# Dense mixture in steps of 768 tokens, with sums of block products formed in PSUM

## The chip, the cores and the metric

One core of a Trainium2 chip (trn2). The metric is the time of one execution on the device in microseconds (us); the median of three runs of the kernel before is 754.18 us (754.17 to 754.35). Five engines work side by side, each through its own queue in program order, and wait for each other by semaphores: TensorE (PE, matmuls), VectorE (DVE), ScalarE (ACT), GpSimd (POOL) and SyncE (SP, which issues transfers). PEld is the load of the stationary operand of a matmul. PE writes only to PSUM, which has eight banks of 512 f32 values for each of 128 partitions; DVE and ACT read it from there.

## The reference

Three layers in a row on 1536 tokens of 512 numbers: an attention with a local window and a few global keys, a mixture of 8 experts in which each token goes to one, and a dense mixture, in which each token goes through all 4 experts. The change touches the last one alone:

```python
def _moe2_ref(x, domain_probs, w1, w2):          # x 1536x512, w1 4x512x1024, w2 4x1024x512
    p = domain_probs / (domain_probs.sum(-1, keepdims=True) + 1e-09)
    out = np.zeros((N, D), dtype=np.float32)
    for e in range(E):
        h = np.maximum(x @ w1[e], 0.0)
        out += p[:, e:e + 1] * (h @ w2[e])
    return out
```

## The kernel before, in words

Everything runs in the order in which it is written; the whole body is under a hand-made schedule. The dense mixture begins at L770.

**Exactness.** A product of two f32 matrices is made of three matmuls on numbers split into a high part (rounded to fp32r) and a low part, the rest: high x high, high x low, low x high (`mm3`, L108 to L111). Every operand is therefore split: ACT copies the high part, and DVE or POOL subtracts it (`sub_lo`, L68).

**First layer by seven products.** The hidden layer is computed in 16 quarters: q counts them, q // 4 is the expert, and a quarter has 256 of its 1024 hidden units. For one quarter, the 512 x 256 weights are cut into four blocks A11, A12, A21, A22, and the tokens (two halves of 768) by the two halves of the 512 features into four blocks as well. Instead of eight block products, seven are made (Strassen's scheme in Winograd's form), from sums S1 to S4 of weight blocks and sums T1 to T4 of token blocks. The products are A11 B11, A12 B21, S4 B22, A22 T4, S1 T1, S2 T2, S3 T3. The kernel after numbers them 1 to 7 in this order, and the texts below use these numbers. Each product is 6 matmuls (`product`, L829: three matmuls for each of two halves of the features). The sums that need all tokens' blocks (T1 to T4) are made once, by `prep_a` to `prep_d` (L797 to L827), in the first steps; the sums of weights (S1 to S4) for each q by POOL (`sums_moe2`, L596), and the weights are split by `split_moe2` (L604): ACT makes the high parts, POOL the low ones, for "a" (the A blocks), "s" (their sums) and "w" (second layer).

**Steps.** A step takes one quarter q and one column c of 256 tokens of each half, so 512 tokens: 42 matmuls of 256 columns. There are 16 x 3 = 48 steps (L861). In the first six, c is the outer loop and q alternates between 0 and 1, so that tokens can be prepared as they are needed: tiles 2 and 3 in step 1, tiles 4 and 5 in step 3 (`preps`, L862). From step 6 on q is the outer loop.

**What a step does** (L880 to L956): four products go into `pf` and three into `pg` (two PSUM tiles of two banks each). ACT copies three of the products to SBUF (`sf`, L896), DVE forms `uv`, the sums `cc` (L897, L898, L914, L923), ACT makes the high part of the positive values `hh` (L938) and DVE their low part `hl` (L939). Between the products PE makes the second layer of the step before it (`second`, L837): four times 6 matmuls of 512 columns, each a tile of 128 tokens, whose result is added to the output with its share by DVE (L857), or, for q = 0, written by ACT (L855). In steps 0 to 5 all seven products come first (L32), then the second layer of the step before.

**Weights.** Two sets of buffers alternate by q (L594). After the last step of q the A blocks of q + 2 are fetched into its buffers and summed by POOL (L953 to L955); one step later they are split, in the middle of that step, right behind `uv` and `cc` (L899 to L902), and two steps later the second layer's weights "w".

Of the kernel before, what the change touches and what calls it, by code (L numbers as in the profile page):

```python
# [8 lines left out]
F32 = mybir.dt.float32  # L9
# [5 lines left out]
ALU = mybir.AluOpType  # L15
# [16 lines left out]
ORDERS = {i: ((0, 1, 3, 2, 4, 5, 6) if i % 2 else (0, 4, 1, 3, 2, 5, 6), ()) for i in range(6)}  # L32
# [12 lines left out]
def attention_moe_moe(ctx: ExitStack, tc: tile.TileContext, qkv, nints_d, wg, w1, w2, dprob, u1, u2, out):  # L45
# [62 lines left out]
    def mm3(o, ah, al, bh, bl, start, stop):  # L108
        nc.tensor.matmul(o, ah, bh, start=start, stop=False)  # L109
        nc.tensor.matmul(o, ah, bl, start=False, stop=False)  # L110
        nc.tensor.matmul(o, al, bh, start=False, stop=stop)  # L111
# [658 lines left out]
    with ExitStack() as c2:  # L770
# [6 lines left out]
        sf = placed("sf", [P, 3, 256], F32, 0)  # L777
        uv = placed("uv", [P, 256], F32, 3072)
        cc = placed("cc", [P, 4, 256], F32, 4096)
        hhs = [placed(f"hh{n}x", [P, 4, 256], F32R, 8192 + 8192 * n) for n in range(2)]  # L780
        hls = [placed(f"hl{n}x", [P, 4, 256], F32R, 12288 + 8192 * n) for n in range(2)]
# [47 lines left out]
        def product(o, buf, a, b, c):  # L829
            cs = slice(c * 256, (c + 1) * 256)  # L830
            n = (a % 4) * 256
            lo, hi = (buf[0][1], buf[3][1]) if a < 4 else (buf[2][1], buf[4][1])
            for d in range(2):
                wc = slice(n + d * P, n + (d + 1) * P)
                mm3(o, hi[:, wc], lo[:, wc], xh[:, b, d, cs], xl[:, b, d, cs], d == 0, d == 1)

        def second(q, c, hs, n):  # L837
            buf = bufs2[q % 2]
            hh, hl = hs
            ac = next_pa()  # L840
            half, k = divmod(n, 2)
            tc_ = slice(k * P, (k + 1) * P)
            tt = half * NI + 2 * c + k
            e = q // NQ
            nc_ = 2 if (q, c, n) == (NQ * E2 - 1, 2, 3) else 1
            for j in range(nc_):
# [3 lines left out]
                for fh in range(2):  # L850
                    i = 2 * fh + half
                    wc = slice(fh * 512 + cs.start, fh * 512 + cs.stop)
                    mm3(ac[:, cs], hh[:, i, tc_], hl[:, i, tc_], buf[5][1][:, wc], buf[1][1][:, wc], fh == 0, fh == 1)
# [7 lines left out]
        steps = [(q, c) for c in range(3) for q in range(2)] + [(q, c) for q in range(2, NQ * E2) for c in range(3)]  # L861
# [18 lines left out]
        for i, (q, c) in enumerate(steps + [(None, None)]):  # L880
            tt = nc.vector.tensor_tensor
            order = ORDERS.get(i, ((0, 1, 2, 3), (4, 5, 6)))
            js = preps.get(i)
            if q is not None:
                buf = bufs2[q % 2]
                pf = ps.tile([P, 4, 256], F32, name="pf")
                pg = ps.tile([P, 3, 256], F32, name="pg")
                hh, hl = hhs[i % 2], hls[i % 2]
                prods = [(pf[:, 0], A11, B11), (pf[:, 1], S1, T1), (pf[:, 2], S3, T3), (pf[:, 3], S2, T2),
                         (pg[:, 0], A12, B21), (pg[:, 1], S4, B22), (pg[:, 2], A22, T4)]  # L890
                for n in order[0]:
                    if i == 0 and n == 1:
                        for _ in range(NFILL):
                            nc.tensor.matmul(pf[:, 1], wz[:, 0:P], wz, start=True, stop=True)
                    product(prods[n][0], buf, *prods[n][1:], c)
                nc.scalar.activation(out=sf, in_=pf[:, 0:3], func=AF.Copy)  # L896
                tt(out=uv, in0=pf[:, 3], in1=sf[:, 0], op=ALU.add)  # L897
                tt(out=cc[:, 3], in0=sf[:, 1], in1=sf[:, 2], op=ALU.add)  # L898
                for d, what in ((2, "w"), (1, "as")):  # L899
                    if i >= d and steps[i - d][1] == 2 and steps[i - d][0] + 2 < NQ * E2:  # L900
                        for wh in what:
                            split_moe2(bufs2[steps[i - d][0] % 2], wh, ("A", "G"))  # L902
            if js:
                prep_b(js[0])
                prep_c1(js[0])
                prep_c2(js[0], nc.gpsimd)
                prep_t4(js[0])
            if pend is not None:
                second(*pend, 0)
                second(*pend, 1)  # L910
            if q is not None:
                for n in order[1]:
                    product(prods[n][0], buf, *prods[n][1:], c)
                tt(out=cc[:, 0:3], in0=pg, in1=sf, op=ALU.add)  # L914
            if js:
                prep_b(js[1])
                prep_c1(js[1])
                prep_c2(js[1], nc.gpsimd)
                prep_t4(js[1])
            last = i == len(steps) - 1  # L920
            for n, (what, engs) in enumerate(PD):
                if n == 1 and q is not None and not last:
                    tt(out=cc[:, 1:4], in0=cc[:, 1:4], in1=uv.unsqueeze(1).to_broadcast([P, 3, 256]), op=ALU.add)  # L923
                for j, eng in zip(js or (), engs):
                    prep_d(j, what, eng)
            if i + 1 in preps:
                for t in (preps[i + 1][0], preps[i + 1][0] + NI):
                    prep_a(t)
            if last:
# [10 lines left out]
            if i == 2:  # L940
                gather_x(5 + NI)
# [224 lines left out]
```

## Time and profile before

| | before |
|---|---|
| median of the runs | 754.18 us |
| the profiled execution: time | 756.36 us |
| the profiled execution: span, first to last instruction | 754.6 us |
| PE busy | 98% of the span |
| DVE, ACT, POOL busy | 69%, 41%, 33% |
| share of the dense mixture | from about 239 us to the end |

The rows of the trace are of one profiled execution, with times in us from the start of its span; its time is 1.8 us longer than the span and 2.2 us longer than the median of the runs without a profile. A busy PE is one with a matmul on its way: the records of two neighbouring matmuls overlap, so how fast they follow each other is read from their starts, not from their durations. The granted clock (PEclk) is the share of full speed that TensorE was given in a stretch: 1.00 is its level of 2.4 GHz, 0.5 that of 1.2 GHz.

### The profile page before, as it was taken

To read this page: it belongs to the slowest core of one execution; us is meant where nothing else is said; L and a number is where in the kernel's file an instruction comes from. 1 tells how busy PE (TensorE), PEld (TensorE's weight loads), DVE (VectorE), ACT (ScalarE), POOL (GpSimd) and SP (SyncE) were. 2 spreads that over 40 slices of the span, in tenths; PEclk is the share of its full clock that TensorE was granted. 3 is DMA by queue.
4 is the path that set the end of the run, shared out by engine and by line. 5 is a ranking of instruction groups with operands and counts; after the bars stand their busy time and mean duration, and the time that the engine had idled before them with its cause. 6 is when DMAs were issued, how large, how long until landed. Compare 5 with 4: busy or idle time off the path is not lost.

```text
span 754.6 us, 12189 instructions
## 1 busy us (share of the span) xinstructions
PE 736.4 (98%) x4794; PEld 657.3 (87%) x4794; DVE 522.1 (69%) x1024; ACT 312.7 (41%) x489; POOL 252.8 (33%) x244
## 2 busy tenths in 40 slices
PE   8999998999999999999999999999999999999996
PEld 7999997777777898899999999999999999999995
DVE  7777863678769888576666666676666666666665
ACT  4878861687855544513223132232222322213110
POOL 5666631000046604724414244141341523415000
PEclk8999996999999999999999999999999999999999
DMA  6867602999931300200001000010000100011013
GB/s 163 277 220 247 215 21 86 387 364 405 342 103 54 99 16 28 84 29 29 29 29 56 29 29 29 29 56 29 30 29 29 56 28 29 34 38 43 1 43 129
DMA packets 36018, 74.87 MB, mean 99 GB/s; under 512 B 15960, under 2 KB 16216, under 8 KB 35954
## 3 DMA queue, kind: packets, MB, share of 16 engines
q1 hardware_dynamic: 34034, 69.39, 26.7%
q0 software_dynamic: 1920, 4.64, 1.9%
q8 instruction: 39, 0.64, 0.3%
q14 instruction: 25, 0.20, 0.1%
HBM read 65.19 MB, written 10.49 MB: 100 GB/s over the span
## 4 chain that ended last, share of the span: by engine, by line
PE 87%; DVE 5%; DMA 3%; issue 2%; ACT 2%; POOL 0%; POOLq 0%; ACTq 0%; DVEq 0%
PE pf L110 6%; PE pf L109 6%; PE pf L111 6%; PE pg L109 4%; PE pg L110 4%; PE pg L111 4%; PE pa0x L111 3%; PE pa0x L109 3%; PE pa1x L110 3%; PE pa0x L110 3%; PE pa1x L109 3%; PE pa3x L109 3%; PE pa3x L111 3%; PE pa1x L111 3%; PE pa3x L110 3%; PE pa2x L111 3%
## 5 line engine op out<-in xcount | busy, mean ns | idle before, releaser
L914 DVE TENSOR_TENSOR cc<-pg,sf 128x768 f32<-128x768 f32 x48 | 45.9, 957 | 57.0 <-PE pg L111 55.6
L896 ACT ACTIVATE sf<-pf 128x768 f32<-128x768 f32 x48 | 39.0, 813 | 107.5 <-PE pf L111 107.5
L938 ACT ACTIVATE hh0x<-cc 128x1024 fp32r<-128x1024 f32 x24 | 25.5, 1060 | 120.5 <-DVE cc L923 117.8
L938 ACT ACTIVATE hh1x<-cc 128x1024 fp32r<-128x1024 f32 x23 | 24.4, 1060 | 106.6 <-DVE cc L923 106.6
L599 POOL TENSOR_TENSOR w6x<-w4x 128x256 f32<-128x256 f32 x8 | 9.4, 1178 | 175.1 <-DMA w4x<-in_u_dram 93.2
L923 DVE TENSOR_TENSOR cc<-cc,uv 128x768 f32<-128x768 f32 x47 | 52.5, 1117 | 1.6
L939 DVE SCALAR_TENSOR_TENSOR hl0x<-cc,hh0x 128x1024 fp32r<-128x1024 f32 x24 | 29.5, 1231 | 24.8 <-ACT hh0x L938 24.8
L939 DVE SCALAR_TENSOR_TENSOR hl1x<-cc,hh1x 128x1024 fp32r<-128x1024 f32 x23 | 28.5, 1241 | 25.0 <-ACT hh1x L938 25.0
L897 DVE TENSOR_TENSOR uv<-pf,sf 128x256 f32<-128x256 f32 x48 | 20.4, 424 | 34.1 <-ACT sf L896 34.1
L110 PE MATMUL pf<-xl,r8x 128*128 128x256 f32 x144 | 40.8, 283 | 2.7 <-DVE xl L68 2.5
L857 DVE SCALAR_TENSOR_TENSOR xr<-pa2x,pr,xr 128x512 f32<-128x512 f32 x44 | 33.0, 750 | 13.4 <-PE pa2x L111 13.4
L109 PE MATMUL pf<-xh,r8x 128*128 128x256 f32 x144 | 40.6, 282 | 0.0
L111 PE MATMUL pf<-xh,r6x 128*128 128x256 f32 x144 | 40.4, 281 | 0.0
L109 PE MATMUL pf<-xh,r14x 128*128 128x256 f32 x144 | 40.4, 281 | 0.0
L110 PE MATMUL pf<-xl,r14x 128*128 128x256 f32 x144 | 40.4, 281 | 0.0
L111 PE MATMUL pf<-xh,r12x 128*128 128x256 f32 x144 | 40.4, 281 | 0.0
L599 POOL TENSOR_TENSOR w12x<-w10x 128x256 f32<-128x256 f32 x8 | 8.9, 1119 | 92.6 <-DMA w10x<-in_u_dram 92.6
L857 DVE SCALAR_TENSOR_TENSOR xr<-pa1x,pr,xr 128x512 f32<-128x512 f32 (+1 forms) x46 | 33.9, 737 | 2.2 <-PE pa1x L111 2.2
L857 DVE SCALAR_TENSOR_TENSOR xr<-pa0x,pr,xr 128x512 f32<-128x512 f32 (+1 forms) x46 | 33.9, 736 | 1.2 <-PE pa0x L111 1.2
L857 DVE SCALAR_TENSOR_TENSOR xr<-pa3x,pr,xr 128x512 f32<-128x512 f32 x45 | 33.5, 744 | 0.6 <-PE pa3x L111 0.6
L110 PEld LDWEIGHTS pf<-xl,r8x 128*128 128x128 f32 x144 | 27.0, 188 | 3.4 <-issue 2.5
L68 POOL TENSOR_TENSOR r11x<-w11x,r15x 128x1024 fp32r<-128x1024 f32 x7 | 17.0, 2424 | 35.8 <-ACT r15x L97 35.8
(1189 smaller groups left out, 2700.2 us busy)
## 6 DMA issues: line engine op xcount, KB each, us to landing
w4x<-in_u_dram SPq DMA_DIRECT2D x8, 512.0 KB, 3.2
w5x<-in_u_dram SPq DMA_DIRECT2D x8, 512.0 KB
w10x<-in_u_dram SPq DMA_DIRECT2D x8, 512.0 KB, 3.9
w11x<-in_u_dram SPq DMA_DIRECT2D x8, 512.0 KB, 3.4
qk1x<-in_qkv_dram SPq DMA_DIRECT2D x6, 512.0 KB, 4.7
vv<-in_qkv_dram SPq DMA_DIRECT2D x12, 256.0 KB, 4.9
out_dram<-xr SPq DMA_DIRECT2D x11, 256.0 KB, 2.0
qk0x<-in_qkv_dram SPq DMA_DIRECT2D x5, 512.0 KB, 4.2
```

Of the source, the lines that this page charges most:

```text
L68: eng.tensor_tensor(out=lo, in0=src, in1=hi.bitcast(F32), op=ALU.subtract)
L109: nc.tensor.matmul(o, ah, bh, start=start, stop=False)
L110: nc.tensor.matmul(o, ah, bl, start=False, stop=False)
L111: nc.tensor.matmul(o, al, bh, start=False, stop=stop)
L599: eng.tensor_tensor(out=sm[:, 0], in0=a21, in1=a22, op=ALU.add)
L857: nc.vector.scalar_tensor_tensor(out=acc[:, tt, cs], in0=ac[:, cs], scalar=pr[:, tt, e:e + 1], in1=acc[:, tt, cs], op0=ALU.mult, op1=ALU.add)
L896: nc.scalar.activation(out=sf, in_=pf[:, 0:3], func=AF.Copy)
L897: tt(out=uv, in0=pf[:, 3], in1=sf[:, 0], op=ALU.add)
L914: tt(out=cc[:, 0:3], in0=pg, in1=sf, op=ALU.add)
L923: tt(out=cc[:, 1:4], in0=cc[:, 1:4], in1=uv.unsqueeze(1).to_broadcast([P, 3, 256]), op=ALU.add)
L938: nc.scalar.activation(out=hh, in_=cc, func=AF.Relu)
L939: nc.vector.scalar_tensor_tensor(out=hl, in0=cc, scalar=0.0, in1=hh.bitcast(F32), op0=ALU.max, op1=ALU.subtract)
```

## The change: what it does

From step 6 on a step takes 384 tokens of each half in place of 256, so 768 in all: 28 such steps in place of 42, two for each q. The first six steps keep 256. Each has the same seven products of 6 matmuls, now 256 or 384 columns wide, and a second layer of four or six times 6 matmuls of 512 columns.

The four PSUM tiles are used differently. Products 1, 6, 7 and 4 are added up in one bank (two such banks, by turns of the step), 5 and 3 in another, 2 has one of its own. After 1, after 5 and after 6 ACT copies the bank as it stands (`part`); after 3, 7 and 2 DVE adds a copy to the bank as it stands; after 4 the bank itself is the result. As each quarter of the hidden values is known, ACT makes its high part (`high`), and DVE its low part one piece of work later (`lows`). A product that adds to a bank can only start when the reader of the bank before it is done.

The order of a step is written as a string: digits are products, "s" one sixth or one fourth of the second layer of the step before, "p" the preparation of one tile of tokens, "f" eight matmuls that fill a gap. The splits of the weights now stand behind the whole string of a step.

```diff
-ORDERS = {i: ((0, 1, 3, 2, 4, 5, 6) if i % 2 else (0, 4, 1, 3, 2, 5, 6), ()) for i in range(6)}
+WC = 3 * P
+SEQS = {0: "12f56374", 1: "1563pss724pss", 2: "12s56s37s4s", 3: "1563pss724pss", 4: "12s56s37s4s", 5: "15s63s72s4s", 6: "12s56s37s4s"}
+SEQ = "15s63ss72s4ss"
...
+        banks = [ps.tile([P, 512], F32, name=f"pb{n}x") for n in range(4)]
+        parts = xp.tile([P, 3, WC], F32, name="parts")
...
-        def second(q, c, hs, n):
+        def second(q, tok, w, hs, n):
...
-            half, k = divmod(n, 2)
+            half, k = divmod(n, w // P)
+            half = 1 - half
...
-        steps = [(q, c) for c in range(3) for q in range(2)] + [(q, c) for q in range(2, NQ * E2) for c in range(3)]
+        MS = {1: (A11, B11), 2: (A12, B21), 3: (S4, B22), 4: (A22, T4), 5: (S1, T1), 6: (S2, T2), 7: (S3, T3)}
+
+        class Step:
+            def __init__(self, i, q, tok, w, last):
+                self.buf, self.cs, self.late = bufs2[q % 2], slice(tok, tok + w), []
+                x, y, z = banks[i % 2], banks[2], banks[3]
+                self.bank = {n: b[:, 0:w] for n, b in ((1, x), (6, x), (7, x), (4, x), (2, y), (5, z), (3, z))}
+                self.part, self.cc, self.hs = parts[:, :, 0:w], ccs[w], hps2[w][i % 2]
+
+            def high(self, half, fs, src):
+                nc.scalar.activation(out=self.hs[0][:, half, fs], in_=src, func=AF.Relu)
+                self.late.append((half, fs, src))
+
+            def lows(self, late):
+                for half, fs, src in late:
+                    nc.vector.scalar_tensor_tensor(out=self.hs[1][:, half, fs], in0=src, scalar=0.0, in1=self.hs[0][:, half, fs].bitcast(F32),
+                                                   op0=ALU.max, op1=ALU.subtract)
...
+            def mul(self, n):
+                o, part, cc = self.bank[n], self.part, self.cc
+                late = self.take()
+                product(o, self.buf, *MS[n], self.cs, n in (1, 2, 5), True)
+                add = lambda j, p: nc.vector.tensor_tensor(out=cc[:, j], in0=o, in1=part[:, p], op=ALU.add)
+                if n in (1, 5, 6):
+                    nc.scalar.activation(out=part[:, (1, 5, 6).index(n)], in_=o, func=AF.Copy)
+                elif n == 3:
+                    add(0, 2)
+                elif n == 7:
+                    add(1, 1)
+                    self.high(1, slice(0, 2), cc[:, 0:2])
+                elif n == 2:
+                    add(2, 0)
+                    self.high(0, 0, cc[:, 2])
+                else:
+                    self.high(0, 1, o)
+                self.lows(late)
+
+        steps = [(q, c * 256, 256, c == 2) for c in range(3) for q in range(2)]
+        steps += [(q, c * WC, WC, c == 1) for q in range(2, NQ * E2) for c in range(2)]
...
+        for i, st in enumerate(steps + [None]):
+            js = list(preps.get(i, ()))
+            fs = list(range(2 * pend[2] // P)) if pend else []
+            step = st and Step(i, *st)
+            for m in SEQS.get(i, SEQ) if st else "s" * len(fs):
+                if m == "s":
+                    late = step.take() if st else []
+                    second(*pend, fs.pop(0))
+                    if st:
+                        step.lows(late)
+                elif m == "f":
...
+                elif m == "p":
+                    j = js.pop(0)
+                    prep_b(j)
+                    prep_c1(j)
+                    prep_c2(j, nc.gpsimd)
+                    prep_t4(j)
+                    if not js:
+                        for what, engs in PD:
+                            for j, eng in zip(preps[i], engs):
+                                prep_d(j, what, eng)
+                else:
+                    step.mul(int(m))
+            if st:
+                step.lows(step.take())
                 for d, what in ((2, "w"), (1, "as")):
-                    if i >= d and steps[i - d][1] == 2 and steps[i - d][0] + 2 < NQ * E2:
+                    if i >= d and steps[i - d][3] and steps[i - d][0] + 2 < NQ * E2:
                         for wh in what:
                             split_moe2(bufs2[steps[i - d][0] % 2], wh, ("A", "G"))
...
+            for n, t in enumerate(preps.get(i + 1, ())):
+                if (i, n) == (2, 1):
+                    gather_x(5 + NI)
+                prep_a(t)
+                prep_a(t + NI)
             if i == 8:
                 count(xp, next_pa()[:, 0:E1])
...
+            if pend and pend[0] + 2 < NQ * E2 and steps[i - 1][3]:
+                fetch_moe2(pend[0] + 2, bufs2[pend[0] % 2], "w")
+            if st:
+                q, tok, w, last = st
+                if last and q + 2 < NQ * E2:
+                    fetch_moe2(q + 2, step.buf, "a")
+                    sums_moe2(step.buf, nc.gpsimd)
+                pend = (q, tok, w, step.hs)
```

## Rows read from the trace of the kernel before

**Rows 1.** The page's busy time by engine: us (share of the span) and instructions.

```profile
PE 736.4 (98%) x4794; PEld 657.3 (87%) x4794; DVE 522.1 (69%) x1024; ACT 312.7 (41%) x489; POOL 252.8 (33%) x244
```

**Rows 2.** Busy time by stretch: the stretch, its length, busy us of PE, PEld, DVE, ACT, POOL (instructions), granted clock, share of the DMA engines, GB/s.

```profile
340.00:720.00 380.00, 380.00 (x2413) 345.62 (x2413) 248.85 (x331) 101.19 (x121) 120.45 (x94) 1.00 0.10 33
...
748.00:754.60 6.60, 0.00 (x0) 0.00 (x0) 0.28 (x1) 0.00 (x0) 0.00 (x0) 0.72 0.26 88
```

**Rows 3.** What PE waited for from 238 us to the end: us in total, times, longest us.

```profile
PE pf L110 <- DVE xl L68: 2.5, 3, 0.9
PE pa1x L281 <- DVE t40x L821: 0.5, 1, 0.5
```

**Rows 4.** ACT's reads of the first PSUM tile in steps 9 and 47, from the timeline: start us, duration us, and in brackets the idle time before and what ended it.

```profile
340.08 0.81 ACT L896 ACTIVATE sf<-pf 128x768 f32<-128x768 f32 x1 [2.74 <-PE pf L111]
...
734.77 0.81 ACT L896 ACTIVATE sf<-pf 128x768 f32<-128x768 f32 x1 [2.56 <-PE pf L111]
```

**Rows 5.** The timeline within step 13: the first of twelve 512-wide matmuls, ACT's read of the tile that PE has just finished, the first of eighteen 256-wide matmuls, and the first 512-wide one after them.

```profile
381.37 0.39 PE L109 MATMUL pa1x<-r9x,hh0x 128*128 128x512 f32 x1
...
381.63 0.81 ACT L896 ACTIVATE sf<-pf 128x768 f32<-128x768 f32 x1 [2.22 <-PE pf L111]
...
384.09 0.28 PE L109 MATMUL pg<-xh,r7x 128*128 128x256 f32 x1
...
386.21 0.39 PE L109 MATMUL pa3x<-r9x,hh0x 128*128 128x512 f32 x1
```

**Rows 6.** PE's timeline in step 2, from the first of twelve 256-wide matmuls soon after a wait to the 512-wide one behind them; and in step 3 two groups of four transposes, 128 columns wide.

```profile
264.72 0.28 PE L109 MATMUL pg<-xh,r8x 128*128 128x256 f32 x1
...
266.08 0.39 PE L109 MATMUL pa0x<-r15x,hh1x 128*128 128x512 f32 x1
...
276.48 0.60 PE L281 MATMUL pa0x<-ident,xr 128*128 128x128 f32 x4
276.92 0.60 PE L281 MATMUL pa1x<-ident,xr 128*128 128x128 f32 x4
```

**Rows 7.** Groups of equal instructions: line, engine, operation, out<-in, count, busy us, mean ns of one, idle us before. DVE from 335 to 700 us, and ACT's reads of 512 and of 256 columns from 235 to 330 us.

```profile
L914 DVE TENSOR_TENSOR cc<-pg,sf 128x768 f32<-128x768 f32 x36 | 34.5, 958 | 49.3 <-PE pg L111 47.9 <-PE pa2x L233 1.4
L857 DVE SCALAR_TENSOR_TENSOR xr<-pa1x,pr,xr 128x512 f32<-128x512 f32 x35 | 26.0, 742 | 0.0
L939 DVE SCALAR_TENSOR_TENSOR hl0x<-cc,hh0x 128x1024 fp32r<-128x1024 f32 x18 | 22.1, 1226 | 20.3 <-ACT hh0x L938 20.3
L897 DVE TENSOR_TENSOR uv<-pf,sf 128x256 f32<-128x256 f32 x35 | 14.9, 425 | 24.4 <-ACT sf L896 24.4
...
L808 ACT ACTIVATE xh<-pa1x 128x512 fp32r<-128x512 f32 x5 | 3.0, 598 | 5.6 <-PE pa1x L281 5.4 <-PE pa1x L239 0.2
...
L826 ACT ACTIVATE xh<-t40x 128x256 fp32r<-128x256 f32 x3 | 1.2, 408 | 0.4 <-DVE t40x L821 0.4
```

**Rows 8.** The timeline of the first steps: PE at the wait in step 0, the last high part (ACT) and the last low part (DVE) of the tokens prepared ahead of step 0, and the first matmul of steps 1 to 5.

```profile
243.21 0.38 PE L110 MATMUL pf<-xl,r8x 128*128 128x256 f32 x1 [0.70 <-DVE xl L68]
...
243.86 0.42 ACT L826 ACTIVATE xh<-t41x 128x256 fp32r<-128x256 f32 x1
...
245.12 0.41 DVE L68 TENSOR_TENSOR xl<-t41x,xh 128x256 fp32r<-128x256 f32 x1
...
247.20 0.39 PE L109 MATMUL pf<-xh,r13x 128*128 128x256 f32 x1
...
260.05 0.28 PE L109 MATMUL pf<-xh,r7x 128*128 128x256 f32 x1
...
271.53 0.28 PE L109 MATMUL pf<-xh,r13x 128*128 128x256 f32 x1
...
283.73 0.28 PE L109 MATMUL pf<-xh,r7x 128*128 128x256 f32 x1
...
295.27 0.28 PE L109 MATMUL pf<-xh,r13x 128*128 128x256 f32 x1
```

**Rows 9.** ACT's timeline in step 5: the high parts of A (two pieces) and of S for q = 2, and the evacuation of the last second product of the step.

```profile
299.06 0.93 ACT L97 ACTIVATE r7x<-w4x 128x512 fp32r<-128x512 f32 x2
299.89 1.05 ACT L97 ACTIVATE r8x<-w6x 128x1024 fp32r<-128x1024 f32 x1
...
305.85 0.69 ACT L855 ACTIVATE xr<-pa3x,pr 128x512 f32<-128x512 f32 x1 [0.50 <-PE pa3x L111]
```

**Rows 10.** POOL's groups from 297 to 325 us (columns as in rows 7): the low parts of S and of the two pieces of A for q = 2; and PE's first matmul of step 6 from the timeline.

```profile
L68 POOL TENSOR_TENSOR r6x<-w6x,r8x 128x1024 fp32r<-128x1024 f32 x1 | 2.4, 2402 | 0.0
...
L68 POOL TENSOR_TENSOR r4x<-w4x,r7x 128x256 fp32r<-128x256 f32 x1 | 1.5, 1460 | 0.1
L68 POOL TENSOR_TENSOR r4x<-w4x,r7x 128x512 fp32r<-128x512 f32 x1 | 1.3, 1302 | 3.1 <-PE pg L111 3.1
...
305.65 0.28 PE L109 MATMUL pf<-xh,r7x 128*128 128x256 f32 x1
```

**Rows 11.** Busy time by stretch in the attention layer (columns as in rows 2; the granted clock is the third number from the end).

```profile
112.50:116.00 3.50, 3.24 (x17) 3.14 (x17) 1.50 (x9) 0.00 (x0) 0.00 (x0) 0.51 0.30 78
116.00:119.00 3.00, 2.39 (x12) 1.58 (x11) 1.43 (x9) 0.12 (x1) 0.19 (x1) 0.50 0.00 0
119.00:126.00 7.00, 6.47 (x31) 6.41 (x32) 1.82 (x13) 0.48 (x1) 2.19 (x3) 0.50 0.04 14
```

More of the change, by code (lines that the diff above doesn't have):

```diff
@@ L106, in attention_moe_moe, with mm3 @@
     SCH_M1 = [("A", "V")]
[L108 to L111, printed above, removed]
+    def mm3(o, ah, al, bh, bl, start, stop, **kw):
+        nc.tensor.matmul(o, ah, bh, start=start, stop=False, **kw)
+        nc.tensor.matmul(o, ah, bl, start=False, stop=False, **kw)
+        nc.tensor.matmul(o, al, bh, start=False, stop=stop, **kw)
     ordered = ExitStack()
@@ L776, in attention_moe_moe @@
         t4 = [xp.tile([P, 2, P], F32, name=f"t4{n}x") for n in range(2)]
[L777 to L781, printed above, removed]
+        banks = [ps.tile([P, 512], F32, name=f"pb{n}x") for n in range(4)]
+        parts = xp.tile([P, 3, WC], F32, name="parts")
+        places = {256: (3072, 11264), WC: (20480, 4608)}
+        ccs = {w: placed(f"cc{w}x", [P, 3, w], F32, 0) for w in places}
+        hps2 = {w: [[placed(f"h{m}{n}{w}x", [P, 2, 2, w], F32R, places[w][n] + 16 * w * (m == "l")) for m in "hl"] for n in range(2)] for w in places}
         acc = xr
@@ L827, in prep_d, with product @@
             sub_lo(eng, xl[:, ps_, :, c], src, xh[:, ps_, :, c])
-        def product(o, buf, a, b, c):
-            cs = slice(c * 256, (c + 1) * 256)
+        def product(o, buf, a, b, cs, start, stop):
             n = (a % 4) * 256
@@ L879, in attention_moe_moe @@
         pend = None
[L880 to L898, printed above, removed]
+        for i, st in enumerate(steps + [None]):
[9 more added lines that the diff above has]
+                elif m == "f":
+                    for _ in range(NFILL):
+                        nc.tensor.matmul(banks[3][:, 0:256], wz[:, 0:P], wz, start=True, stop=True)
+                elif m == "p":
[12 more added lines that the diff above has]
+                step.lows(step.take())
@@ L908, in attention_moe_moe @@
[L908 to L929, printed above, removed]
-                for n in (2, 1):
-                    rows = slice(2 - n, 4, 2)
-                    us = slice(2, 3) if n == 2 else slice(1, 4, 2)
-                    tt(out=cc[:, us], in0=cc[:, us], in1=uv.unsqueeze(1).to_broadcast([P, 3 - n, 256]), op=ALU.add)
-                    nc.scalar.activation(out=hh[:, rows], in_=cc[:, rows], func=AF.Relu)
-                    second(*pend, 4 - n)
-                    nc.vector.scalar_tensor_tensor(out=hl[:, rows], in0=cc[:, rows], scalar=0.0, in1=hh[:, rows].bitcast(F32), op0=ALU.max, op1=ALU.subtract)
-            elif q is not None:
-                nc.scalar.activation(out=hh, in_=cc, func=AF.Relu)
-                nc.vector.scalar_tensor_tensor(out=hl, in0=cc, scalar=0.0, in1=hh.bitcast(F32), op0=ALU.max, op1=ALU.subtract)
```

33 lines of the change are left out of this document (7 added, 26 removed).

## The prediction

> **What bounds the kernel now.** I read the page's busy shares first: TensorE (PE) is busy for 98% of the span, VectorE (DVE) for 69% [rows 1]. A share over the whole span hides stages, so next the busy times by stretch: from 340 to 720 us PE is busy in every microsecond at granted clock 1.00, and in the last 6.6 us it does nothing [rows 2]. Then what PE waited for since the dense mixture began at about 239 us: 3.0 us in four waits [rows 3], of which the stretch from 340 to 720 has none. So from step 6 on this stage is a queue of matmuls without a gap, and its time is count times pitch (the time from one matmul's start to the next one's). The check: ScalarE (ACT) reads the first bank once a step, at 340.08 and, 38 steps later, at 734.77 [rows 4], so a step takes 394.69 / 38 = 10.387 us. The timeline gives twelve 512-wide matmuls from 381.37 to 384.09 and eighteen 256-wide ones from there to 386.21 [rows 5]: pitches 0.2267 and 0.1178 us. A step has 42 and 24 of them: 42 x 0.1178 + 24 x 0.2267 = 10.39 us. It closes, so work taken from DVE or ACT in these steps is worth nothing by itself; only the pitch, or a new wait of PE, moves the end.
>
> **The width of the block products.** The seven products of three matmuls by two halves stay, and the 512-wide second products stay. In steps 6 to 47, 42 x 42 = 1764 matmuls of 256 columns become 28 x 42 = 1176 of 384. No row shows a 384-wide one. Upper bound: the same time per column as a 256-wide one, 1.5 x 0.1178 = 0.1767, worth nothing. Lower bound: the same per column as a 512-wide one, 0.75 x 0.2267 = 0.1700. I take the lower end, for this reason. Behind a wait the same 256-wide matmuls run at 0.1133 (twelve from 264.72 to 266.08), exactly half of the 512-wide pitch, and the 128-wide ones need 0.11 each (four from 276.48 to 276.92) though they stream half as many columns [rows 6]. So something per matmul takes about 0.11 us, most likely the load of the weights, which each of these matmuls has; beside 256 columns it is as long as the stream and the two get in each other's way for 4.5 ns, beside 512 it is hidden. At 384 the stream (0.170) is far longer, so I expect it hidden as at 512. Then a step of 768 tokens takes 42 x 0.170 + 36 x 0.2267 = 15.30 us in place of 1.5 x 10.387 = 15.58; 28 steps give **-7.8 us**. A straight line through 0.1178 and 0.2267 would give 0.172 and -5.3; the upper bound 0. The Trainium skill, "TensorE: Matmul & The Clock Gate", section "Back-to-back issue gap", speaks against the change: a warm matmul costs its columns at 2.4 GHz plus a fixed 2.5 ns, so estimated by that page three matmuls of 256 made two of 384 save only 2.5 ns, about 1.5 us in all. The measured pitches lie above that formula at both widths, so the trace does not bear it out.
>
> **Sums in PSUM.** DVE's four additions (two of 256 columns, two of 768) become three of 384. Per 768 tokens I count for it these three (about 0.56 each, between 425 ns at 256 and 958 at 768), three rests (2.05 together, from 1226 ns at 1024) and six accumulations of 0.74 [rows 7]: 8.2 us of 15.3. That is under today's 65% of DVE [rows 2] and hidden behind PE either way: nothing. What it adds is that PE must wait for a reader before it adds to a bank. The lag from the last matmul to ACT's read is 0.26 us after PE has gone on (381.37 to 381.63 [rows 5]); a copy of 384 takes about 0.5 (408 ns at 256, 598 at 512 [rows 7]). In the order "15s63ss72s4ss" (s: six 512-wide matmuls, 1.36 us; a product 1.02): 6 comes 2.38 us after 1, needs 0.76; 3 likewise after 5; 7 comes 3.7 after 6; 4 comes 2.38 after 7, whose addition needs 0.82, or 1.6 where one accumulation is ahead of it on DVE. No wait. The bounds are nothing and a few tenths each step (a rival). The next step uses the other bank of two for 1, 6, 7, 4.
>
> **The first steps (0 to 4, still 256 wide; a product is 0.71 us).** Here the readers stand behind the preparation of the tokens. Step 0, "12f56374": 5 waits until 243.21 and ends at about 243.9, as before [rows 8]. 6 needs ACT's copy of 1, which is queued behind the T4 copies (243.86 + 0.42): 244.6. Next on ACT is the Relu of 1+2, which waits for DVE's addition behind the subtraction of 245.12 (0.41): 245.9, Relu to 246.35, and only then the copy of 5, 246.7, for which 3 waits. 7 ends at 248.1; 4 waits for DVE to add 7 (0.26 + 0.42) and ends at 249.55, where step 1 began at 247.20: +2.35. Steps 1 and 3 have no long wait left: seven products, four s, two sets of transposes (0.88 each): 12.15, against 12.85 and 12.20 (starts in [rows 8]). Steps 2 and 4 lose the wait for xl of 0.9 us [rows 3], since T3 now comes later in the order, and gain about 0.15 for a copy of 1 that stands behind six preparation copies and two evacuations: 10.54 against 11.48 and 11.54. Sum: 2.35 - 0.7 - 0.94 - 0.05 - 1.0 = **-0.3**. It rests on chains of small pieces; I give it 1.5 either way.
>
> **Where the weights of q = 2 come late.** The split of A and S for q = 2 is needed first in step 6. Before, ACT did it in the middle of step 5, at 299.06, right behind its read of the bank, and PE began step 6 at 305.65 without a wait [rows 9, 10]. Now it is written behind the whole of step 5, so on ACT it stands behind the evacuation of the last second product, which began at 305.85 and took 0.69 [rows 9]. Both engines are in order. So PE is done at T, ACT evacuates from T + 0.2 to 0.9, splits the first half of A to T + 1.5, POOL subtracts 1.30 [rows 10] to T + 2.8, plus some 0.1 of hand-over; two of six matmuls (0.34) can go before: wait 2.6 us. All PE work queues behind it. S follows POOL's 1.46 and 2.40 and is 0.3 to 0.4 late for product 5. The split of w for q = 2 goes from mid step 6 to its end: Relu, ACT 1.05, POOL 2.4 end about 4.2 us after product 4, and the first s of step 7 wants it 3.6 after: 0.6. Together **+3.5**. Later weights have a whole step between the split and their use (q + 2 follows two steps of q + 1): nothing. Their copies (0.93 and 1.05 [rows 9]) run under the last two s of a step.
>
> **The sum.** -7.8 - 0.3 + 3.5 = -4.6 us. The profiled execution took 756.36 us, its span 754.6; I expect a span of 750.0. The runs' median of 754.18 is 2.2 below the profiled time; less 4.6 it is **749.5**. The tail (last accumulation, last store) is the same.
>
> **Rivals.** A, forecast: 0.62, by itself 747.8 to 751.5. B, step 6 does not wait, or under 1 us: the gain stands alone, 746.0. For it: product 2 and an s were put early in step 6; against: the first product needs the split. 0.12. C, the 2.6 us gap lowers PE's clock: the attention layer has 13.5 us at granted clock near 0.5 [rows 11]; all of it in dense work would cost 6.8, while waits of 0.9 [rows 3] kept 1.00; say 3, so 752.5. 0.07. D, product 4 waits in each step for DVE's addition of 7: 0.1 us is 28 x 0.1 = 2.8 and gives 752.3, and from 0.16 us a step on the gain is gone; 0.3 gives 757.9. Against it the slack of 0.8 or more above. 0.08. E, slower: the 4.5 ns goes with columns, not with the crowded weight load, so 384 keeps 0.1767 and only the late split is left: 754.18 - 0.3 + 3.5 = 757.4; it decides against the change from a pitch of 0.174 up. For it: most 256-wide matmuls run at 0.1178 with no wait anywhere near; against: 0.1133 behind waits. 0.11. By the formula of the Trainium skill, "TensorE: Matmul & The Clock Gate", section "Back-to-back issue gap" (estimate: 1.5 us saved), the time would be 755.9.
>
> **How the numbers follow.** A change of about 0.2% (1.5 us) is what a measurement of this kernel can tell from none. Faster by more (under 752.7): A, B, half of C, a little of D: 0.76. Within: rest of C, part of D, the edge of A: 0.10. Slower (above 755.7): E and the heavy end of D: 0.14. The range goes from B to the light end of D and a pitch between the bounds: 746.0 to 754.6; E and the rest of D lie outside.
>
> **What would show it.** Right: 384-wide starts 0.170 apart; steps of 15.3 us from step 7 on; one PE wait of 2 to 3 us at about 305.4 on a POOL subtraction of r4 and a short one at step 7's first s; step 1 beginning 2 to 2.5 us later, step 5 at about the same time. Wrong: a pitch of 0.174 or more, a PE wait that comes back in each step, granted clock below 1.00 behind 305 us, or a step 6 that starts on time.

## The result: slower, and where the time went

The kernel after takes **759.82 us** (median of 22 runs, 756.93 to 767.03) against 754.26 for the kernel before beside it (median of 22): a ratio of 1.0072, 95% interval 1.0054 to 1.0090. The forecast was 749.5, with a range of 746.0 to 754.6. The runs after form two groups: 10 lie between 756.93 and 757.67 us, at mean clocks of 0.984 to 0.987, and 12 from 759.75 up, at 0.971 to 0.982. The profiled execution is of the second group: 761.62 us, span 759.8.

The page of the kernel after, busy time by engine (answers to [rows 1]):

```profile
PE 739.2 (97%) x4206; PEld 660.1 (87%) x4206; DVE 451.6 (59%) x986; ACT 330.3 (43%) x596; POOL 240.5 (32%) x244
```

PE has 588 matmuls fewer and is busy for 2.8 us longer. DVE fell from 69% to 59%. The busy times by stretch (columns as in [rows 2]):

```profile
244.00:252.00 8.00, 7.06 (x34) 6.77 (x35) 4.25 (x8) 2.17 (x7) 6.15 (x6) 0.57 0.61 192
306.00:314.00 8.00, 5.62 (x20) 4.75 (x19) 0.56 (x1) 3.47 (x6) 5.96 (x6) 0.79 0.36 133
340.00:720.00 380.00, 380.00 (x1906) 345.92 (x1905) 194.12 (x293) 114.32 (x195) 116.42 (x97) 1.00 0.10 33
```

In the long stretch PE is as full as before, at granted clock 1.00. In two short ones, where the kernel before had 1.00, the clock is down: a mean of 0.57 over 8 us is 6.9 us at half, the lower level, and 0.79 is 3.4 us.

ACT's first read of a bank in step 8 and in step 33, the last one, from the timeline (answers to [rows 4]):

```profile
340.93 0.49 ACT L891 ACTIVATE parts<-pb0x 128x384 f32<-128x384 f32 x1 [2.40 <-PE pb0x L113]
...
730.57 0.49 ACT L891 ACTIVATE parts<-pb1x 128x384 f32<-128x384 f32 x1 [3.35 <-PE pb1x L113]
```

25 steps in 389.64 us are 15.586 us each; as many tokens before, one and a half steps, were 1.5 x 10.387 = 15.580. The steady steps gained nothing. In counts and pitches below, a block product is one matmul of the products 1 to 7 (256 or 384 columns wide, into a bank `pb`), and a second product one matmul of the second layer (512 columns, into a bank `pa`). PE's timeline in one of the steps (answers to [rows 5]): the first of twelve 384-wide block products, of six 512-wide second products, of six block products, and the next second product.

```profile
394.81 0.34 PE L111 MATMUL pb1x<-xh,r8x 128*128 128x384 f32 x1
...
396.93 0.39 PE L111 MATMUL pa0x<-r9x,hh0384x 128*128 128x512 f32 x1
...
398.29 0.34 PE L111 MATMUL pb1x<-xh,r7x 128*128 128x384 f32 x1
...
399.35 0.39 PE L111 MATMUL pa1x<-r9x,hh0384x 128*128 128x512 f32 x1
```

Twelve in 2.12 us and six in 1.06: a pitch of **0.1767**, as good as 1.5 x 0.1178. The 512-wide pitch is still 1.36 / 6 = 0.2267. Then what PE waited for from 235 us to the end (columns as in [rows 3]):

```profile
PE pb0x L111 <- ACT r7x L99: 1.3, 1, 1.3
PE pb0x L113 <- POOL r4x L70: 1.1, 1, 1.1
PE pb3x L111 <- ACT parts L891: 1.1, 1, 1.1
PE pb3x L112 <- DVE xl L70: 0.7, 1, 0.7
PE pb0x L111 <- ACT parts L891: 0.5, 1, 0.5
PE pb0x L111 <- DVE cc256x L889: 0.5, 1, 0.5
PE pa0x L112 <- POOL r5x L70: 0.3, 1, 0.3
```

All seven are in steps 0, 6 and 7. No later step waits for a reader of a bank. Step 0 in PE's timeline: product 6 and product 3 behind a wait for a copy, product 4 behind DVE's addition, the first matmul of step 1, and the first one at full pitch again:

```profile
242.37 0.39 PE L111 MATMUL pb0x<-xh,r8x 128*128 128x256 f32 x1 [0.53 <-ACT parts L891]
...
244.42 0.39 PE L111 MATMUL pb3x<-xh,r8x 128*128 128x256 f32 x1 [1.07 <-ACT parts L891]
...
247.61 0.58 PE L111 MATMUL pb0x<-xh,r7x 128*128 128x256 f32 x1 [0.52 <-DVE cc256x L889]
...
249.06 0.42 PE L111 MATMUL pb1x<-xh,r13x 128*128 128x256 f32 x1
...
251.61 0.28 PE L111 MATMUL pb1x<-xh,r14x 128*128 128x256 f32 x1
```

From 249.06 to 251.61 there are twelve matmuls, 0.2125 us apart in place of 0.1178: TensorE is at its lower level. And the start of step 6, from the timelines of PE, ACT and POOL: the last second product of step 5, its evacuation, the high parts of A, the low ones, and the matmuls that waited; the last two rows are the first of six block products and the second product behind them.

```profile
305.89 0.39 PE L113 MATMUL pa3x<-r9x,hl0256x 128*128 128x512 f32 x1
...
306.32 0.69 ACT L855 ACTIVATE xr<-pa3x,pr 128x512 f32<-128x512 f32 x1 [0.97 <-PE pa3x L113]
...
306.90 0.93 ACT L99 ACTIVATE r7x<-w4x 128x512 fp32r<-128x512 f32 x2
...
307.58 0.45 PE L111 MATMUL pb0x<-xh,r7x 128*128 128x384 f32 x1 [1.29 <-ACT r7x L99]
...
307.96 2.08 POOL L70 TENSOR_TENSOR r4x<-w4x,r7x 128x512 fp32r<-128x512 f32 x2 [7.08 <-issue]
...
309.28 0.44 PE L113 MATMUL pb0x<-xh,r4x 128*128 128x384 f32 x1 [1.08 <-POOL r4x L70]
...
310.47 0.52 PE L111 MATMUL pb2x<-xh,r7x 128*128 128x384 f32 x1
...
312.39 0.63 PE L111 MATMUL pa0x<-r15x,hh1256x 128*128 128x512 f32 x1
```

This is the chain that the prediction drew, piece by piece: PE, evacuation, high part, POOL, PE. What its sum did not have is the clock: the six block products from 310.47 to 312.39 stand 0.320 us apart in place of 0.1767, at the lower level.

### The profile page after: what moved, and what is told of

Same layout as the page of the kernel before. It is cut to its first block, busy times and chain, and to the rows that moved or that the text cites. A ratio compares the mean times of both kernels' runs of the same rounds, so it can differ in the third digit from the quotient of the medians.

```text
span 759.8 us, 11192 instructions
## 1 busy us (share of the span) xinstructions
PE 739.2 (97%) x4206; PEld 660.1 (87%) x4206; DVE 451.6 (59%) x986; ACT 330.3 (43%) x596; POOL 240.5 (32%) x244
## 4 chain that ended last, share of the span: by engine, by line
PE 91%; DVE 2%; ACT 1%; issue 1%; POOL 0%; ACTq 0%; POOLq 0%
PE pa2x L111 3%; PE pa2x L113 3%; PE pa2x L112 3%; PE pa3x L113 3%; PE pa3x L111 3%; PE pa3x L112 3%; PE pa1x L111 3%; PE pa0x L112 3%; PE pa0x L113 3%; PE pa0x L111 3%; PE pa1x L113 3%; PE pa1x L112 3%; PE pb0x L113 3%; PE pb0x L111 3%; PE pb3x L111 3%; PE pb0x L112 3%
## 5 line engine op out<-in xcount | busy, mean ns | idle before, releaser
L873 ACT ACTIVATE hh0384x<-cc384x 128x384 fp32r<-128x384 f32 (+1 forms) x28 | 19.2, 686 | 71.8 <-DVE cc384x L889 71.8
L873 ACT ACTIVATE hh1384x<-cc384x 128x768 fp32r<-128x768 f32 (+1 forms) x28 | 19.2, 687 | 71.3 <-DVE cc384x L889 71.3
L70 POOL TENSOR_TENSOR r5x<-w5x,r9x 128x1024 fp32r<-128x1024 f32 x7 | 16.8, 2400 | 75.8 <-ACT r9x L99 75.8
L70 POOL TENSOR_TENSOR r10x<-w10x,r13x 128x512 fp32r<-128x512 f32 (+1 forms) x16 | 16.9, 1056 | 61.9 <-PE pa3x L113 61.2
L111 PE MATMUL pb3x<-xh,r8x 128*128 128x384 f32 (+1 forms) x68 | 22.7, 334 | 1.1 <-ACT parts L891 1.1
L112 PE MATMUL pb3x<-xl,r8x 128*128 128x384 f32 (+1 forms) x68 | 22.6, 332 | 0.7 <-DVE xl L70 0.7
L111 PE MATMUL pb3x<-xh,r14x 128*128 128x384 f32 (+1 forms) x68 | 22.7, 334 | 0.0
L113 PE MATMUL pb3x<-xh,r6x 128*128 128x384 f32 (+1 forms) x68 | 22.6, 332 | 0.0
L112 PE MATMUL pb3x<-xl,r14x 128*128 128x384 f32 (+1 forms) x68 | 22.6, 332 | 0.0
L113 PE MATMUL pb3x<-xh,r12x 128*128 128x384 f32 (+1 forms) x68 | 22.5, 332 | 0.0
```

Of the source, the lines that this page charges most:

```text
L70: eng.tensor_tensor(out=lo, in0=src, in1=hi.bitcast(F32), op=ALU.subtract)
L111: nc.tensor.matmul(o, ah, bh, start=start, stop=False, **kw)
L112: nc.tensor.matmul(o, ah, bl, start=False, stop=False, **kw)
L113: nc.tensor.matmul(o, al, bh, start=False, stop=stop, **kw)
L873: nc.scalar.activation(out=self.hs[0][:, half, fs], in_=src, func=AF.Relu)
```

## The experiments

Two questions stood open: what the width is worth, and what the stalls in steps 0 and 6 cost. Since the clock in the layers ahead also differs from execution to execution, I compare, beside the medians, how long the dense mixture took in each profiled execution, from its first block product to the start of its last matmul. The steps of m2_order and m1b_widths, the last two rows, are those of the kernel after; the matmuls that these runs add stand behind them.

| kernel | from, us | to, us | length | against before |
|---|---|---|---|---|
| before | 239.62 | 747.49 | 507.87 | |
| after | 237.39 | 752.94 | 515.55 | +7.68 |
| x_split | 237.10 | 747.50 | 510.40 | +2.53 |
| x_fill | 237.93 | 749.11 | 511.18 | +3.31 |
| x_both | 237.75 | 745.38 | 507.63 | -0.24 |
| x_512 | 238.84 | 746.88 | 508.04 | +0.17 |
| x_256 | 240.75 | 753.16 | 512.41 | +4.54 |
| x_lump | 243.65 | 751.90 | 508.25 | +0.38 |
| m2_order | 239.27 | 750.62 | 511.35 | +3.48 |
| m1b_widths | 237.71 | 752.29 | 514.58 | +6.71 |

### x_split: the weights of q = 2 split in mid-step again

```diff
-SEQS = {... 5: "15s63s72s4s", 6: "12s56s37s4s"}
+SEQS = {... 5: "15s63ws72s4s", 6: "12s56sw37s4s"}
...
+                elif m == "w":
+                    splits()
```

(`splits` holds the loop of splits, unchanged; the other steps still call it at their end.)

> The changed kernel with the splits of the weights of q = 2 (steps 5 and 6 only) put back into the middle of their steps. Theory A (the late split costs 2.6 + 0.6 us of waiting and, through it, a fall of PE's clock that the profile shows at 309.6 us for 3.4 us, so 1.7 more): 3 to 5 us below the changed kernel, so about 754 where the clock did not fall in step 0 either and 757.5 where it did. Rival (steps from 7 on cost more than before): no change beyond 1 us.

Measured: 754.95 us (12 runs, 751.77 to 763.99; 754.5 without the longest one), ratio to before 1.0009 (0.9981 to 1.0038). The waits of steps 6 and 7 are gone; those of step 0 are all still there. The busy times by stretch of its profile:

```profile
244.00:252.00 8.00, 7.36 (x36) 7.07 (x37) 4.51 (x9) 2.13 (x6) 5.72 (x6) 0.57 0.63 198
...
306.00:314.00 8.00, 8.00 (x44) 7.53 (x43) 2.86 (x5) 4.54 (x9) 3.58 (x5) 1.00 0.36 131
```

The clock fall behind step 0 remains, the one behind step 6 is gone with the wait there. With the first of them 757.5 had been expected; this execution took 755.39, and its mixture began 2.5 us earlier than before.

### x_fill: idle matmuls in the gaps of step 0

```diff
-SEQS = {0: "12f56374", ...
+SEQS = {0: "12f5F6GG37F4", ...
...
+                elif m in "FG":
+                    for _ in range(4):
+                        nc.tensor.matmul(banks[1][:, 0:256], wz[:, 0:P], wz, start=True, stop=True)
```

> The changed kernel with 4, 8 and 4 idle matmuls of 256 columns (0.5, 0.9 and 0.5 us, shorter than or as long as PE's three waits there) in step 0, into a bank that is not yet used. Their results are not used. Theory A (step 0's waits let PE's clock fall for 6.8 us in about half of the executions): no fall after 238 us and up to step 5, the times around 761.8 vanish, 757.3 to 759 are left. Rival (the clock falls for another reason, or the spread of the times comes from the attention layer): the two groups of times stay.

Measured: 758.08 us (6 runs, 756.95 to 762.71), ratio 1.0065 (1.0042 to 1.0088). The fillers took the place of three of the four waits of step 0; those of steps 6 and 7 stay as in the kernel after. The stretch behind step 0 in its profile:

```profile
244.00:252.00 8.00, 7.83 (x63) 7.32 (x63) 5.56 (x11) 3.23 (x9) 6.14 (x7) 1.00 0.57 178
```

The clock stays at 1.00, here and, in this execution, behind step 6 as well, although the waits there are unchanged. The times from 761 up did not wholly vanish: five of the six runs lie between 756.95 and 759.49, one at 762.71, at a mean clock of 0.978. Step 1 begins at 247.97 us, 10.04 us after the first product, where the kernel after took 249.06 - 237.39 = 11.67.

### x_both: both edits

> Both edits together: the splits of steps 5 and 6 in mid-step, and the idle matmuls in step 0. Theory A (nothing gained from the width; all of the loss in the late split and in step 0 with the clock): one group of times at 753.5 to 754.5, so like the kernel before within 0.2%. Rival (a price in each of the 28 steps): 756 or more.

Measured: **754.19 us** (12 runs, 753.36 to 755.48), ratio 1.0001 (0.9992 to 1.0010). All that PE waited for in the mixture, and the stretch of step 0:

```profile
PE pb3x L112 <- DVE xl L70: 0.7, 1, 0.7
```

```profile
244.00:252.00 8.00, 7.83 (x63) 7.28 (x62) 5.31 (x11) 3.45 (x9) 6.03 (x6) 1.00 0.58 176
```

With both stalls mended, the change is worth nothing: 28 steps of 768 tokens cost what 42 steps of 512 did. The four lengths of the mixture give the parts of the loss: x_both -0.24; the late split 511.18 - 507.63 = 3.55; the clock fall behind step 0 510.40 - 507.63 = 2.77; what is left of the +7.68, 1.60, I put down to the clock fall behind step 6, which by its length cost about 3.4 / 2 = 1.7. By the medians the late split is worth 758.08 - 754.19 = 3.9 and the fillers, once the split is mended, 0.8 (0.3 without the longest run of x_split). The 12 runs of x_both stay within 2.1 us, at mean clocks of 0.984 to 0.988; 12 of the 22 of the kernel after had a lower one.

### m1b_widths: the pitch of block products at six widths

Behind the output of the kernel after stand streams of 48 matmuls each, so its time of 881.38 us is no kernel's time.

```diff
+        def prods(bank, w, at=0):
+            for j in range(8):
+                product(bank[:, 0:w], buf, (0, 1, 3, 4, 5, 6, 7, 0)[j], j % 7, slice(at, at + w), True, True)
+
+        prods(banks[0], 256)
+        prods(banks[1], 384)
+        prods(banks[2], 512)
+        prods(banks[3], 384, 384)
+        prods(banks[0], 320)
+        prods(banks[1], 448)
+        prods(banks[2], 128)
...
```

> The changed kernel with streams of 48 matmuls each added behind its last step, in which PE waits for nothing: block products of 256, 384, 512, 384 (second half of the tokens), 320, 448 and 128 columns; second products cut to 512, 384 and 256 columns; then 384- and 512-wide ones with a single stationary operand, and 384-wide ones with the operands exchanged between the token and the weight buffers. Their results are not used. Theory 1 (width decides: only the full 512 columns run at the lower price per column): 256 at 0.118 us, 384 at 0.177, 512 at 0.227 in block products and in second products alike. Theory 2 (the operands decide: reading the token blocks is slower per column than reading weights): block products of 512 at 0.236, second products of 384 at 0.170. Theory 3 (the recorded guess, the load of the weights beside the stream): a single stationary operand changes nothing, 128 at 0.11, and 384 in a stream without waits 0.170.

The first matmul of each stream in PE's timeline, and of the one behind them:

```profile
752.41 0.29 PE L111 MATMUL pb0x<-xh,r13x 128*128 128x256 f32 x1
...
757.87 0.33 PE L111 MATMUL pb1x<-xh,r13x 128*128 128x384 f32 x1
...
766.19 0.39 PE L111 MATMUL pb2x<-xh,r13x 128*128 128x512 f32 x1
...
777.39 0.34 PE L111 MATMUL pb3x<-xh,r13x 128*128 128x384 f32 x1
...
785.71 0.31 PE L111 MATMUL pb0x<-xh,r13x 128*128 128x320 f32 x1
...
792.75 0.37 PE L111 MATMUL pb1x<-xh,r13x 128*128 128x448 f32 x1
...
802.45 0.22 PE L111 MATMUL pb2x<-xh,r13x 128*128 128x128 f32 x1
...
807.76 0.44 PE L111 MATMUL pb3x<-r15x,hh1384x 128*128 128x512 f32 x1
```

The difference of two starts by 48: 384 takes 0.1733 twice, 512 takes 0.2333, 320 takes 0.1467, 448 takes 0.2021, 128 takes 0.1106. At 256 the start is ragged; from its third matmul on (752.66) it is 5.21 / 46 = 0.1133. So 384 has a second, lower pitch too, 0.1733, but 0.1700 appears nowhere. At the lower clock level 384 columns took 0.320 us (step 6 above), one column per cycle of 1.2 GHz. An estimate from that for 2.4 GHz is 0.1067, 0.1600 and 0.2133 us at 256, 384 and 512: the rest is 6.7, 13.3 and 20 ns. It grows with the width instead of being hidden by it. Second products ran at 0.2284 in a stream of their own, cut to 384 columns at 0.1739 and to 256 at 0.1197, so none of the three theories came out whole. Streams of 384 with one stationary operand, or with other operands, ran at 0.173 to 0.177 as well. But each of their matmuls still has a load of weights in the trace, so they don't tell whether the rest comes from that load.

### m2_order: which of the two pitches, and when

```diff
+        for j in range(8):
+            sec(banks[0], j)
+            six(banks[1], 384, j)
...
+        sec(banks[0], 0)
+        for j in range(16):
+            six(banks[1], 384, j)
+        wait()
+        for j in range(16):
+            six(banks[2], 384, j)
+        sec(banks[0], 0)
+        for j in range(16):
+            six(banks[1], 256, j)
+        wait()
+        for j in range(16):
+            six(banks[2], 256, j)
```

`sec` is six second products, `six` the six block products of one product; `wait` is three copies on ACT and one 128-wide matmul that reads the last of them (L987). Again these streams follow the output.

> The changed kernel with more PE work behind its last step (results not used): 8 times one second product (6 x 512) and one block product of 384; the same with 256; one second product and 16 block products of 384 in a row; a wait of PE and the 16 again; one second product and 16 block products of 256; a wait and the 16 again. The streams before gave 0.1733 at 384 and 0.1133 at 256 where the steps give 0.1767 and 0.1178. Theory 1 (second products between the block products put them on the dearer pitch, and it stays until PE waits): 0.1767 and 0.1178 in the first, second, third and fifth stretch, 0.1733 and 0.1133 behind the waits. Theory 2 (the steps' other engines cost the difference): 0.1733 and 0.1133 in all of them.

By turns with second products, 384 ran at 0.1767 and 256 at 0.1178. Then, in PE's timeline, 96 matmuls of 384 behind one group of second products, the odd one, 96 more; and the same with 256:

```profile
788.02 0.34 PE L111 MATMUL pb1x<-xh,r13x 128*128 128x384 f32 x1
...
804.98 0.22 PE L987 MATMUL pb3x<-xh,hh0384x 128*128 128x128 f32 x1
...
805.26 0.33 PE L112 MATMUL pb2x<-xl,r13x 128*128 128x384 f32 x1
...
821.73 0.40 PE L111 MATMUL pb0x<-r15x,hh1384x 128*128 128x512 f32 x1
...
823.12 0.28 PE L111 MATMUL pb1x<-xh,r13x 128*128 128x256 f32 x1
...
834.42 0.22 PE L987 MATMUL pb3x<-xh,hh0384x 128*128 128x128 f32 x1
...
834.65 0.28 PE L112 MATMUL pb2x<-xl,r13x 128*128 128x256 f32 x1
...
845.44 0.39 PE L111 MATMUL pb0x<-r15x,hh1384x 128*128 128x512 f32 x1
```

16.96 / 96 = 0.1767, then 16.47 / 95 = 0.1734; 11.30 / 96 = 0.1177, then 10.79 / 95 = 0.1136. The dearer pitch holds for all 96 matmuls behind second products, and is gone behind one odd matmul. That one is not the wait that I had meant it to be: the copies had been made early, and the profile shows no wait of PE there. So the first theory holds for the streams behind second products, but it isn't a wait that ended the dear pitch here. Nor is the rule without exceptions: in m1b_widths the first stream stood right behind second products (256 wide, the last of the mixture) and ran at 0.1133 from its third matmul on, and in step 0 of the kernel after matmuls behind a wait ran at 0.1178. What sets the pitch inside TensorE stays open.

This run says something of the clock as well. PE waits in its mixture as in the kernel after, for the same seven things and as long, yet in its profile both stretches have full clock:

```profile
244.00:252.00 8.00, 6.16 (x47) 5.73 (x48) 5.61 (x12) 2.95 (x8) 6.37 (x6) 1.00 0.47 141
306.00:314.00 8.00, 6.12 (x31) 5.53 (x32) 2.03 (x3) 3.52 (x7) 6.73 (x6) 1.00 0.36 133
```

Its mixture took 511.35 us, 4.20 less than in the profile of the kernel after. In m1b_widths, again the same mixture, both stretches have 0.79, so 3.4 us at half in each, and it took 514.58. The two falls therefore come in some executions and not in others, behind the same waits.

### x_lump: all products of a step first, then all second products

```diff
-SEQ = "15s63ss72s4ss"
+SEQ = "1563724ssssss"
```

With the edits of x_both.

> Both edits of x_both, and from step 7 on all seven products in a row, then the six second products (1563724ssssss). Theory 1 (only runs of products behind a wait are cheap): 0.1767 as in x_both, and a short wait of product 4 for DVE's addition, under 0.2 us a step: 754 to 760. Theory 2 (mixing the two kinds costs): 0.1733 in the runs of 42, so 28 x 42 x 0.0033 = 3.9 us less: 750.3 plus those waits.

PE's timeline: the first of the 42 block products of a step, the first of its 36 second products, the first of the next step:

```profile
401.03 0.34 PE L111 MATMUL pb0x<-xh,r13x 128*128 128x384 f32 x1
...
408.45 0.39 PE L111 MATMUL pa3x<-r9x,hh1384x 128*128 128x512 f32 x1
...
416.61 0.34 PE L111 MATMUL pb1x<-xh,r13x 128*128 128x384 f32 x1
```

7.42 / 42 = 0.1767 and 8.16 / 36 = 0.2267: one run of products and one of second products per step in place of four of each, and the same price. So it isn't the change from one kind to the other that costs, and this order is as good as the other. PE waited for no reader even so. The time, 758.51 us (10 runs, 752.64 to 760.87; ratio 1.0026, 0.9996 to 1.0057), says nothing clear; in its profile the attention layer had a clock of 0.72 from 50 to 68 us, where the kernel before had 1.00, and the mixture took 508.25 us.

### x_512: block products of 512 and 256 columns by turns

```diff
-WC = 3 * P
+WC = 4 * P
...
-        steps += [(q, c * WC, WC, c == 1) for q in range(2, NQ * E2) for c in range(2)]
+        steps += [st for q in range(2, NQ * E2) for st in ((q, 0, WC, False), (q, WC, 256, True))]
```

With the edits of x_both, and with the buffers placed anew for the wider tiles; a step has the order "15s63s72s4s" at 512 and "1s5s6s3ss7s2s4s" at 256.

> Both edits of x_both, and from step 6 on steps of 512 and of 256 tokens of each half by turns in place of 384 and 384. Theory 1 (width decides): 14 x 42 block matmuls of 512 and as many of 256 columns take 588 x (0.2267 + 0.1178) = 202.6 us in place of 1176 x 0.1767 = 207.8, so 5.2 us below x_both: about 749. Theory 2 (reading the token blocks is dear at any width): 0.236 + 0.118, no gain: 754.

755.27 us (12 runs, 753.96 to 759.04, three of them above 758 at a mean clock of 0.980), ratio 1.0017 (0.9996 to 1.0038). From its timeline, the first of twelve 512-wide block products, the first of six second products behind them, and the next block product:

```profile
430.02 0.39 PE L111 MATMUL pb0x<-xh,r7x 128*128 128x512 f32 x1
...
432.82 0.39 PE L111 MATMUL pa1x<-r15x,hh1256x 128*128 128x512 f32 x1
...
434.20 0.39 PE L111 MATMUL pb0x<-xh,r8x 128*128 128x512 f32 x1
```

2.80 / 12 = 0.2333, where two of 256 cost 2 x 0.1178 = 0.2356. The second products' 0.2267, from which I had worked out 0.170, is not what block products cost at that width. And even second products are dearer here, 1.38 / 6 = 0.2300: here the price of a matmul goes by its neighbours too.

### x_256: the change without its width

```diff
-SEQ = "15s63ss72s4ss"
+SEQ = "15s63s72s4s"
...
-        steps += [(q, c * WC, WC, c == 1) for q in range(2, NQ * E2) for c in range(2)]
+        steps += [(q, c * 256, 256, c == 2) for q in range(2, NQ * E2) for c in range(3)]
```

> The changed kernel with 256 tokens of each half in all 48 steps, so the sums in PSUM and the new order alone; the late split of q = 2 and step 0 stay as changed. Theory A (the width of 384 neither gains nor loses, sums in PSUM cost nothing): block matmuls at 0.1178 us, PE without a wait from step 8 on, the same two groups of times as the changed kernel, 757 and 762. Rival (the new sums cost a wait in each step, which only the longer steps hide): a wait that comes back in each step, 760 or more in the lower group.

762.3 us (4 runs, 761.54 to 766.16), ratio 1.0122 (1.0094 to 1.0150): none in the lower of the two groups that I had expected, three near the upper one, one above both. The pitch is 0.1178, and PE waits only in steps 0, 6 and 7, in the last two 1.3 + 1.2 + 0.9; so the rival, a wait in each step, is out. Its profile has no clock fall in the mixture but more of them in the attention layer (0.72 from 50 to 68 us, as in x_lump), so its time is no clean measure. The mixture took 512.41 us; m2_order, also without a clock fall and without fillers but with 384, took 511.35. Of the 1.1 us between them 0.6 is the longer wait in step 7, so the width itself is worth some 0.5 us at most.

## Why the prediction was wrong

**The failed step: the width of the block products.** The term of -7.8 us is 0. The prediction took 0.1700 of the bounds 0.1700 to 0.1767, from the 0.1133 in [rows 6]: the 4.5 ns between 0.1133 and 0.1178 were to be a crowded weight load that a wider stream hides. The runs show another thing: 256 and 384 have two pitches each, 0.1133 and 0.1178, 0.1733 and 0.1767, and in the steps, among second products, both run at the dearer one, which goes with the columns (1.5 x 0.1178 = 0.1767). Even the lower one at 384 is not 0.1700. That figure was 0.75 of a second product's 0.2267, while block products of 512 take 0.2333. The low pitch of [rows 6] was that of a stretch behind a wait, not what a width costs among second products. Rival E had the price (0.1767 kept) and 757.4 us for it, at a chance of 0.11; the lower 10 of the 22 runs, 756.93 to 757.67, lie there. Two of the signs of being wrong that the prediction named came: a pitch of 0.174 or more, and a granted clock below 1.00 behind 305 us.

**The clock.** The prediction gave rival C 0.07, for the gap in step 6 alone. It came, 3.4 us at half clock, and cost about 1.6. It was not the larger one: the waits of step 0, which the sum had at their own length, were followed by 6.9 us at half clock, worth 2.77. Nothing in the prediction looked for that; [rows 3] had single waits of up to 0.9 at full clock, and step 0 now has 0.70, 0.53 and 1.07 us of waiting within 4.2 us, and 0.52 later. The two groups of runs fit executions without and with these falls, by their mean clocks and by their distance (about 4.4 us; 4.20 between the mixtures of m2_order and of the kernel after). But of the 22 runs only one has a profile, so for the others it isn't shown where the clock fell. That the waits bring the falls about is likely and not shown outright: none of the four profiles with fillers (x_fill, x_both, x_512, x_lump) has a fall behind step 0, three of the five without have one (the kernel after, x_split, m1b_widths), and two have not (m2_order, x_256).

**The late split: right.** Expected 2.6 at the start of step 6, 0.3 to 0.4 for S, 0.6 at step 7, together 3.5. The waits are 1.29 + 1.08, none and 0.31. What they cost shows in x_fill against x_both: counted from the first block product, x_fill begins step 6 1.50 us later, step 7 2.97 and step 8 3.56. So step 6 lost 2.97 and step 7 0.59. The sum came out; that S cost nothing and the start of step 6 more than 2.6 made up for each other.

**The first steps: right.** Expected +2.35 in step 0 and -0.3 over steps 0 to 4. At full clock (x_fill) step 0 took 10.04 us against 247.20 - 239.62 = 7.58 [rows 8], so +2.46. From the first block product to the first of step 5 it was 295.27 - 239.62 = 55.65 us before, 55.48 in x_both and 55.70 in m2_order, which has no fillers: -0.17 and +0.05. The pieces were further off than the sum, and partly made up for each other: in m2_order steps 1 and 3 took 12.55 and 12.38 us where 12.15 was expected, steps 2 and 4 10.39 each where it was 10.54.

**Sums in PSUM: right.** No step from 8 on waits for a reader, so rival D did not happen; DVE went from 248.85 us of 380 [rows 2] to 194.12, worth nothing, as said.

Measured against its own sum: -7.8 became 0, -0.3 is -0.24 (all of x_both against before), +3.5 is 3.55, and 4.4 of clock stood in no term (4.37 is what is left of the 7.68; m2_order against the kernel after gives 4.20). In the mixture that is 7.7 in place of -4.6. The part ahead of it was 2.23 us shorter in this profile (237.39 against 239.62). That is not the change's: m2_order, with the same program ahead of the mixture, began it at 239.27.

## What to carry to other kernels

Fewer, wider matmuls with the same sum of columns saved nothing here by being fewer, from 256 columns up; take a new width's price from a row in the same neighbourhood, in proportion, until a stream of that width behind the same work says otherwise, and don't read the price of one kind of matmul from another kind. A row that is cheaper behind a wait may say something of the wait, not of the width. Look at the waits of a stretch together, not each by itself, and ask of a cluster of them what it may do to TensorE's clock; a fall can come in one execution and not in the next, so one profile of each kernel doesn't settle it. In x_both, with idle matmuls in the gaps and the split in time, the long runs were gone. And a split moved behind a step costs its whole chain where its first user is the next step.

## What the hardware showed that I had not expected

- Block products have two pitches at full clock, 0.1133 or 0.1178 at 256 and 0.1733 or 0.1767 at 384, and keep one of them over 96 matmuls. The Trainium skill, "TensorE: Matmul & The Clock Gate", section "Back-to-back issue gap", gives 131 ns at 512 columns for a stream of weight loads and matmuls, and for a single one columns at 2.4 GHz and 2.5 ns (by estimate 215.8 at 512, 162.5 at 384). No run here agrees with either: the lowest measured are 226.7 at 512 and 173.3 at 384.
- Block products of 512 columns took 0.2333 us, second products of 512 columns 0.2267 among narrower block products and 0.2300 among 512-wide ones, all at granted clock 1.00.
- In a stream of its own a 128-wide block product costs 0.1106 us, nearly as much as a 256-wide one at its lower pitch (0.1133).
- Behind waits of 0.70, 0.53 and 1.07 us within 4.2 us TensorE spent 6.9 us at its lower level in the kernel after and in x_split, 3.4 in m1b_widths, and none in m2_order and x_256, whose waits were the same. In the four profiles with matmuls in the gaps the level was not lost.
